# Quarter-array token matmuls for the odd 64 tokens, in a fused attention and MLP-mixer kernel

## The chip, the cores and the metric

The kernel runs on one core of a Trainium2 chip. The metric is the device time of one execution in microseconds, the lower the better.

## The reference

Two stages are computed, for 8 batches of 448 tokens (S) with 12 heads of 64 elements, so 768 features (D). All inputs and the output are float32; the kernel works in float16 with float32 sums.

```python
def _attn_ref(q, k, v):
    S = q.shape[2]
    scale = 1.0 / np.sqrt(q.shape[-1])
    scores = scale * np.matmul(q, k.transpose(0, 1, 3, 2)) - np.log(S)
    attn = 1.0 / (1.0 + np.exp(-scores))
    return np.matmul(attn, v)

def _moe_ref(x, w_tok1, w_tok2, w_ch1, w_ch2):    # x: the heads side by side, 8 x 448 x 768
    xt = x.transpose(0, 2, 1)
    h = np.maximum(xt @ w_tok1, 0.0) @ w_tok2     # 448 -> 256 -> 448 tokens
    u = x + h.transpose(0, 2, 1)
    h2 = np.maximum(u @ w_ch1, 0.0) @ w_ch2       # 768 -> 1536 -> 768 features
    return u + h2
```

## The kernel before

Tokens are loaded so that partition p of 64 holds tokens 7p to 7p+6; a "round" i of attention takes one such j of 7 for two heads. 448 tokens are three and a half tiles of 128: blocks 0 to 2 are full, block 3 has only 64 tokens. In the kernel before, even batches keep that half block in partitions 0 to 63 and odd batches in 64 to 127 (`side`, `ORDER`, `x_block`, `w1_slot`), so that two batches' halves lie in one tile `ut` for the last step.

The work of a batch is:

- attention (`attention`): for each of 3 groups of four heads, 7 rounds S (L587, four matmuls of 64 by 64 array tiles each, into a `wide` PSUM tile), a sigmoid per round on ScalarE (L603), then V (L625, 28 such matmuls into two single banks), and a copy to `xT` on ScalarE (L658). From batch 2 on, q, k and x are transposed by DMAs on SP, after POOL has reordered q and k (L503); in batches 0 and 1 TensorE does it instead (L531 for q and k, L678 for x), and so for x of the last group of batches 2 and 3.
- the first token matmul K1 (`token`, L820): blocks 0 to 3 of x against `w_tok1`, 384 features at a time, followed by a relu on VectorE (L832). Block 3 is a full 128-row matmul although half its rows are blank.
- the second token matmul K2 (L850): for each of 4 blocks and 2 halves of the features two matmuls, then the sum with x on VectorE (L871), a cast on ScalarE (L879) and a DMA transpose into `uT`. Block 3 uses a full tile and only 64 of its output rows.
- the first channel matmul C1 (`channel1`, L927): 12 steps of six matmuls with 448 columns, relu on VectorE (L952) into `h2aT`.
- the second channel matmul C2 (`channel2`): for blocks 0 to 2 12 matmuls per half (L992). For block 3 of two batches together 24 matmuls per half with tiles of 128 by 64 (L1001). Then the sum on VectorE (L1015) and the store.

Batch 0 is different: its token matmuls (K1a L710, KT L744) run piece by piece between its attention groups.

The order of the work is written out by a planner (`Plan.run`, `choose`) when the program is built. Each step has an engine, a planned duration, the steps that it follows and the buffers that it uses. For TensorE the planner picks among the candidates that can start first: an attention visit (two rounds S, at times with a V) when it is due, token steps, then C1, then C2. Each engine then runs its own list in that order. There are four single banks of PSUM (`bank`) for V, K1, K2, C1 and C2, and two double ones (`wide`) for S. A "visit" means a stretch in which the array is in 64 by 64 tiles. `fill` matmuls (L482) keep TensorE going in planned gaps of the first 21 us; the planner has its own model of when loads land (`pipe`).

Of the kernel before, what the change touches and what calls it, by code (L numbers as in the profile page):

```python
# [55 lines left out]
class Plan:  # L56
# [4 lines left out]
    def __init__(self, pools):  # L61
# [4 lines left out]
        self.landed, self.pipe = [0.0] * 8, 0.0  # L66

# [63 lines left out]
    def run(self, choose):  # L131
# [9 lines left out]
        while self.left:  # L141
# [30 lines left out]
            if best is None:  # L172
# [5 lines left out]
                    )[:6000]  # L178
# [4 lines left out]
            if e == "LD":  # L183
                far = self.load_far if self.pipe > 50.0 else 0.4
                free["POOL"] = t + o.n * o.issue
                if self.pipe < 8.6 < free["POOL"] + 1.3 + o.us:
                    self.pipe = 9.6
                self.pipe = max(self.pipe, free["POOL"] + 1.3) + o.us
                o.end = self.pipe + far
# [15 lines left out]
def kernel(  # L205
# [27 lines left out]
    FILL, UP = 21.0, 7  # L233

# [16 lines left out]
    w_tok1 = const("w_tok1", [128, J, TT], FP16)  # L251
    w_tok2_s = const("w_tok2_s", [128, 2, S], FP16)
    w_tok2 = const("w_tok2", [128, 2, 14, P], FP16)
# [5 lines left out]
    ORDER = {0: (0, 4, 1, 5, 2, 6, 3), 1: (3, 4, 0, 5, 1, 6, 2)}  # L259
# [6 lines left out]

    def x_block(side, blk):

        return blk if side == 0 else (blk + 1) % 4

    def mm(n):
        return n / 2400 + 0.003
# [16 lines left out]
    blank = [plan.buf(f"xT{i}", 2, [128, 2, 512], FP16, keep=True) for i in (0, 0, 1, 1)]  # L289

    def zero():
        for i, t in enumerate(blank):
            nc.vector.memset(t[:, :, S:512] if i < 2 else t[:, :, 0 : 512 - S], 0.0)
        for i, t in enumerate(u16_tail):
            nc.vector.memset(t[64:128, :] if i % 2 == 0 else t[0:64, :], 0.0)
# [56 lines left out]
    def load_w_tok1(part):  # L352

        view = moe_w_tok1.rearrange("(p j) t -> p j t", j=J)
        moves = (
            ((0, 0, 0, 4), (64, 0, 4, 3), (64, 3, 3, 1)),
            ((0, 4, 4, 3), (64, 4, 0, 3)),
        )[part]
# [7 lines left out]
        a = op(f"ld_tok1_{part}", "LD", 1.3 if part == 0 else 1.0, emit, uses=[w_tok1])  # L366
# [3 lines left out]
    def load_w_tok2():  # L370
# [8 lines left out]
        for a_, z, j, n in ((0, 6, 0, 3), (1, 6, 4, 3), (6, 8, 3, 1), (8, 14, 4, 3), (9, 14, 0, 3)):  # L379

            def spread(a=a_, z=z, j=j, n=n):
# [6 lines left out]
                op(f"spread{a_}", "DVE", 0.45, spread, [b], [w_tok2_s, w_tok2], rank=-1 if a_ < 7 else 2)  # L388
# [39 lines left out]
    tok1_ld = load_w_tok1(0)  # L428
# [4 lines left out]
    tok1_late = load_w_tok1(1)  # L433
# [55 lines left out]
    def turned(b, m, what, side):  # L489
# [3 lines left out]
        if b >= 2:  # L493
            pm = plan.buf(f"{what}p", 2, [128, J, 2, E], FP16, name=f"{what}p_{b}_{m}")

            def permute():
                src = raw.ap().rearrange("r h j e -> r j h e")
                if side == 0:
                    parts = ((slice(0, 5, 2), slice(0, 3)), (slice(1, 6, 2), slice(4, 7)), (slice(6, 7), slice(3, 4)))
                else:  # L500
                    parts = ((slice(2, 7, 2), slice(0, 3)), (slice(1, 6, 2), slice(4, 7)), (slice(0, 1), slice(3, 4)))
# [675 lines left out]
```

## Time and profile before

| | |
|---|---|
| median of 8 runs | 379.3 us (378.75 to 379.97) |
| profiled execution | 379.58 us |
| its span, first to last instruction | 377.8 us |
| TensorE busy | 369.5 us, 3243 matmuls |
| ScalarE busy | 206.0 us |
| VectorE busy | 164.4 us |
| POOL busy | 116.9 us |
| first channel matmul starts | 38.91 us |
| last matmul ends, last instruction ends | 373.8 us, 377.8 us |
| granted TensorE clock | 0.999 |

A group line of the profile reads: line, engine, operation, output<-input, shape, how many | busy us, mean ns of one | idle time before them and who ended it. [...] the rate is read from start to start in the chain or the timeline. A line of waits reads: who waited, for whom, us in total, how often, the longest.

### The profile page before, as it was taken

To read this page: it belongs to the slowest core of one execution; us is meant where nothing else is said; L and a number is where in the kernel's file an instruction comes from. 1 tells how busy PE (TensorE), PEld (TensorE's weight loads), DVE (VectorE), ACT (ScalarE), POOL (GpSimd) and SP (SyncE) were. 2 spreads that over 40 slices of the span, in tenths; PEclk is the share of its full clock that TensorE was granted. 3 is DMA by queue.
4 is the path that set the end of the run, shared out by engine and by line. 5 is a ranking of instruction groups with operands and counts; after the bars stand their busy time and mean duration, and the time that the engine had idled before them with its cause. 6 is when DMAs were issued, how large, how long until landed. Compare 5 with 4: busy or idle time off the path is not lost.

```text
span 377.8 us, 7941 instructions
## 1 busy us (share of the span) xinstructions
PE 369.5 (98%) x3243; PEld 190.2 (50%) x3243; DVE 164.4 (44%) x308; ACT 206.0 (55%) x251; POOL 116.9 (31%) x263
## 2 busy tenths in 40 slices
PE   8899999999999999999999999999999999999995
PEld 4455454554455554554445555444445565555663
DVE  4485336643353423552342434643432266554221
ACT  5886885476747666776674777954654123000000
POOL 8883226344533325443444433530000000000000
PEclk9999999999999999999999999999999999999999
DMA  7999999999967999999999999993113655200344
GB/s 105 175 167 206 208 208 181 127 222 174 136 107 121 158 183 159 111 148 181 171 134 158 163 185 213 177 147 71 30 16 97 103 113 118 52 2 0 85 100 108
DMA packets 97172, 50.25 MB, mean 133 GB/s; under 512 B 70576, under 2 KB 93616, under 8 KB 97136
## 3 DMA queue, kind: packets, MB, share of 16 engines
q1 hardware_dynamic: 72656, 27.62, 43.1%
q0 software_dynamic: 24240, 21.81, 42.8%
q8 instruction: 25, 0.41, 0.5%
q10 hardware_dynamic: 240, 0.31, 0.2%
q14 instruction: 11, 0.09, 0.1%
HBM read 43.84 MB, written 11.01 MB: 145 GB/s over the span
## 4 chain that ended last, share of the span: by engine, by line
PE 87%; DMA 5%; POOL 4%; ACT 1%; DVE 1%; issue 1%; POOLq 0%; ACTq 0%
PE c L927 27%; PE c L992 25%; PE qk L587 10%; PE xa L625 8%; PE yn L850 5%; PE c L1001 4%; PE k L820 4%; DMA qT<-qp 2%; DMA k<-in_k_dram 2%; DMA uT<-u 1%; POOL k L329 1%; PE k L710 1%; PE xb L678 1%; ACT attn L603 1%; PE tq L531 1%
## 5 line engine op out<-in xcount | busy, mean ns | idle before, releaser
L603 ACT ACTIVATE attn<-qk,att_bias 128x896 f16<-128x896 f32 (+1 forms) x172 | 161.8, 988 | 76.8 <-PE qk L587 76.4
L927 PE MATMUL c<-uT,w_ch 128*128 128x448 f16 x576 | 118.3, 353 | 0.4 <-DMA uT<-u 0.4
L992 PE MATMUL c<-w_ch,h2aT 128*128 128x384 f16 x576 | 98.8, 326 | 0.0
L952 DVE TENSOR_SCALAR h2aT<-c 128x448 f16<-128x448 f32 x96 | 60.0, 625 | 80.7 <-PE c L927 80.5
L927 PEld LDWEIGHTS <-w_ch 128*128 128x128 f16 x576 | 52.9, 98 | 57.5 <-issue 13.5
L992 PEld LDWEIGHTS <-h2aT 128*128 128x128 f16 x576 | 55.2, 98 | 39.9 <-issue 4.5
L1015 DVE TENSOR_TENSOR u<-u,c 128x384 f32<-128x384 f32 x48 | 26.6, 554 | 75.2 <-PE c L992 75.2
L587 PE MATMUL qk<-qT,kT 64*64 64x448 f16 x672 | 52.9, 363 | 1.0 <-DMA qT<-qp 0.3
L625 PE MATMUL xa<-attn,v 64*64 64x448 f16 x672 | 36.7, 350 | 0.0
L784 POOL COPY mark<-attn 1x1 f16<-1x1 f16 x54 | 9.7, 179 | 74.7 <-ACT attn L603 74.7
L587 PEld LDWEIGHTS <-kT 64*64 64x64 f16 x672 | 14.8, 104 | 31.0 <-issue 28.4
L871 DVE TENSOR_TENSOR u<-x,yn 128x384 f32<-128x384 f16 x48 | 24.4, 549 | 9.7 <-PE yn L850 9.5
L879 ACT ACTIVATE u<-u 128x768 f16<-128x768 f32 x21 | 17.8, 846 | 19.9 <-DVE u L871 19.8
L503 POOL COPY qp<-q 128x384 f16<-128x384 f16 (+1 forms) x54 | 21.4, 432 | 22.9 <-DMA q<-in_q_dram 14.6
L850 PE MATMUL yn<-h,w_tok 128*128 128x384 f16 x128 | 26.4, 327 | 0.0
L503 POOL COPY kp<-k 128x384 f16<-128x384 f16 (+1 forms) x54 | 21.3, 431 | 16.2 <-DMA k<-in_k_dram 14.1
L658 ACT ACTIVATE xT<-xa 128x448 f16<-128x448 f32 x43 | 21.1, 547 | 9.4 <-PE xa L625 7.3
L625 PEld LDWEIGHTS <-v 64*64 64x64 f16 x672 | 19.4, 107 | 12.1 <-DMA q<-in_q_dram 0.7
L820 PE MATMUL k<-x,w_tok 128*128 128x384 f16 x112 | 20.2, 327 | 0.2 <-DVE x L696 0.2
L832 DVE TENSOR_SCALAR h<-k 128x384 f16<-128x384 f32 x28 | 15.5, 556 | 9.9 <-PE k L820 8.7
L340 POOL DMA_DIRECT2D q<-in_q_dram x21 | 15.1, 720 | 6.4 <-issue 6.4
L850 PEld LDWEIGHTS <-w_tok 128*128 128x128 f16 x128 | 11.0, 98 | 12.0 <-issue 5.5
(63 smaller groups left out, 187.4 us busy)
## 6 DMA issues: line engine op xcount, KB each, us to landing
out_dram<-u SPq DMA_DIRECT2D x48, 192.0 KB, 3.0
k<-in_k_dram POOLq DMA_DIRECT2D x21, 224.0 KB, 5.2
q<-in_q_dram POOLq DMA_DIRECT2D x21, 224.0 KB, 6.0
v<-in_v_dram POOLq DMA_DIRECT2D x21, 224.0 KB, 5.4
w_ch<-in_moe_w_ch_dram POOLq DMA_DIRECT2D x6, 768.0 KB, 18.7
out_dram<-ut SPq DMA_DIRECT2D x6, 192.0 KB, 5.3
v<-in_v_dram POOLq DMA_DIRECT2D x6, 112.0 KB, 4.9
x<-xT SPq DMA_TRANSPOSE x32, 4.5
```

What stands on the lines that cost most here:

```text
L503: nc.gpsimd.tensor_copy(out=pm[:, to, :, :], in_=src[:, fr, :, :])
L587: nc.tensor.matmul(out=ps[64 * s : 64 * s + 64, h, 0:S], lhsT=kT[64 * h : 64 * h + 64, i, s, :], rhs=qT[64 * h : 64 * h + 64, :, s, :], st ...
L603: nc.scalar.activation(out=at[:, hs, :], in_=ps[:, hs, 0:S], func=SIGMOID, bias=bias_t[:, :], scale=att_scale,)
L625: nc.tensor.matmul(out=ps[s](slice(64 * h, 64 * h + 64)), lhsT=vf[64 * s : 64 * s + 64, h, order[i], :], rhs=attn[i][64 * s : 64 * s + 64, ...
L658: nc.scalar.activation(out=xt[:, s, c0 : c0 + S], in_=ps[s](every), func=COPYF)
L820: nc.tensor.matmul(out=ps[:, :], lhsT=w_tok1[:, w1_slot(side, blk), 128 * t : 128 * t + 128], rhs=X[b][:, x_block(side, blk), c], start=(b ...
L850: nc.tensor.matmul(out=ps[:, :], lhsT=w_tok2[:, t, s0 : s0 + 2, :], rhs=h1[b][:, t, c], start=(t == 0), stop=(t == 1),)
L871: nc.vector.tensor_tensor(out=to, in0=x, in1=y, op=ADD)
L927: nc.tensor.matmul(out=to(), lhsT=w_ch1[cb // 4][:, db, 128 * (cb % 4) : 128 * (cb % 4) + 128], rhs=uT[b][:, db, :], start=(db == 0), stop ...
L952: nc.vector.tensor_scalar(out=h2aT[b][:, cb, :], in0=to(), scalar1=0.0, scalar2=None, op0=MAX)
L992: nc.tensor.matmul(out=ps[:, :], lhsT=h2aT[b][:, cb, 128 * blk : 128 * blk + 128], rhs=w, start=(cb == 0), stop=(cb == NCB - 1),)
L1015: nc.vector.tensor_tensor(out=t, in0=t, in1=ps[:, :], op=ADD)
```

## The change

For batches 2 to 7 (`PACK`) the half block of 64 tokens is stored twice as compactly. ScalarE's copy of the second half of the features writes its last 64 tokens 64 columns further on, so that after the transpose block 3 of `X[b]` holds the first 384 features in partitions 0 to 63 and the other 384 in partitions 64 to 127. With that, block 3 of K1 becomes two steps V1 of four 64 by 64 matmuls each, which open the sums of two banks; K1 then adds three full matmuls to each bank. Block 3 of K2 becomes one step V2 of eight 64 by 64 matmuls; the two halves of the 128 inner rows land in two banks, and VectorE adds both to x, in two additions per half of the features.

V1 and V2 are kept in a list `tails`. The planner appends them to an attention visit when they are ready within 0.05 us of it (and then may take the visit 3 us of work earlier), or issues them alone.

All batches now use the even layout, so the second arrangement of the weights (two DMAs, two copies) goes. C1's relu writes blocks 0 to 2 to `h2aT` and the last 64 tokens to `h2odd`, where those of two batches lie side by side: block 3 of C2 then is 12 full-tile matmuls per half. The planner's model of the loads gets three pauses instead of one. The diff, cut to its core:

```diff
+        self.hitch = [(8.6, 1.1), (15.2, 1.0), (21.9, 0.8)]
...
                 free["POOL"] = t + o.n * o.issue
-                if self.pipe < 8.6 < free["POOL"] + 1.3 + o.us:
-                    self.pipe = 9.6
                 self.pipe = max(self.pipe, free["POOL"] + 1.3) + o.us
+                while self.hitch and self.pipe > self.hitch[0][0]:
+                    self.pipe += self.hitch.pop(0)[1]
                 o.end = self.pipe + far
...
+    PACK = range(2, 8)
+    JOIN, PULL, ALONE = 0.05, 3.0, 3.5
+    PAUSE = 1.0
...
-    w_tok2 = const("w_tok2", [128, 2, 14, P], FP16)
+    w_tok2 = const("w_tok2", [128, 2, 8, P], FP16)
...
-    ORDER = {0: (0, 4, 1, 5, 2, 6, 3), 1: (3, 4, 0, 5, 1, 6, 2)}
+    ORDER = (0, 4, 1, 5, 2, 6, 3)
...
-        moves = (
-            ((0, 0, 0, 4), (64, 0, 4, 3), (64, 3, 3, 1)),
-            ((0, 4, 4, 3), (64, 4, 0, 3)),
-        )[part]
+        moves = ((0, 0, 0, 4), (64, 0, 4, 3), (64, 3, 3, 1))
...
-    tok1_late = load_w_tok1(1)
...
-            xt = plan.buf(f"xT{side}", 2, [128, 2, 512], FP16, name=f"xT_{b}_{m}", keep=True)
+            xt = plan.buf("xT", 4, [128, 2, 512], FP16, name=f"xT_{b}_{m}", keep=True)
...
-                        nc.scalar.activation(out=xt[:, s, c0 : c0 + S], in_=ps[s](every), func=COPYF)
-
-                got.append(op(f"xT_{b}_{m}_{s}", eng, 0.58, take, [vo, zero_op], [ps[s], xt], rank=-3))
+                        nc.vector.tensor_copy(out=xt[:, s, 0:S], in_=ps[s](every))
+                        return
+
+                    packed = b in PACK and s == 1
+                    for to, fr in ((0, 0), (S, S - 64)) if packed else ((0, 0),):
+                        n = S - 64 if fr == 0 and packed else S - fr
+                        nc.scalar.activation(
+                            out=xt[:, s, to : to + n], in_=ps[s](every)[:, fr : fr + n], func=COPYF
+                        )
+
+                got.append(op(f"xT_{b}_{m}_{s}", eng, 0.75 if b in PACK and s else 0.58, take, [vo, zero_op], [ps[s], xt], rank=-3))
             cols = head_cols(b, m)
...
+            need = [x for m in range(NQ) for x in x_ops[(b, m)]]
+            for n, c in enumerate(cuts) if b not in PACK else ():
...
+            for t in range(2) if b in PACK else ():
+                pair = [bank(f"k1_{b}_{n}_{t}", [128, DH]) for n in range(2)]
+
+                def odd1(pair=pair, t=t):
+                    for n, c in enumerate(cuts):
+                        for g in range(2):
+                            z = slice(128 * t + 64 * g, 128 * t + 64 * g + 64)
+                            nc.tensor.matmul(
+                                out=pair[n][64 * g : 64 * g + 64, :],
+                                lhsT=w_tok1[64 * n : 64 * n + 64, 3, z],
+                                rhs=X[b][64 * n : 64 * n + 64, 3, c],
+                                start=True,
+                                stop=False,
+                                skip_group_check=True,
+                            )
+
+                odd = op(f"V1_{b}_{t}", "PE", mm(DH), odd1, [*need, tok1_ld], [*pair, X[b], w_tok1, h1[b]])
+                odd.kind = "64"
+                tails.append(odd)
+                for n, c in enumerate(cuts):
+
+                    def tok1(ps=pair[n], c=c, t=t):
+                        for blk in range(3):
+                            nc.tensor.matmul(
+                                out=ps[:, :],
+                                lhsT=w_tok1[:, blk, 128 * t : 128 * t + 128],
+                                rhs=X[b][:, blk, c],
+                                start=False,
+                                stop=(blk == 2),
+                                skip_group_check=True,
+                            )
+
+                    o = op(f"K1_{b}_{n}_{t}", "PE", 3 * mm(DH), tok1, [odd], [pair[n], X[b], w_tok1, h1[b]])
+                    first.append(o)
...
+            if b in PACK and blk == 3:
+                pair = [bank(f"yt_{b}_{n}", [128, DH]) for n in range(2)]
+
+                def odd2(pair=pair):
+                    for t in range(2):
+                        for n in range(2):
+                            for g, c in enumerate(cuts):
+                                z = slice(64 * n, 64 * n + 64)
+                                nc.tensor.matmul(
+                                    out=pair[n][64 * g : 64 * g + 64, :],
+                                    lhsT=w_tok2[z, t, 6, :],
+                                    rhs=h1[b][z, t, c],
+                                    start=(t == 0),
+                                    stop=(t == 1),
+                                )
+
+                o = op(f"V2_{b}", "PE", 2 * mm(DH), odd2, [*relus, *tok2_ld], [*pair, h1[b], w_tok2, utile, u16])
+                o.kind = "64"
+                tails.append(o)
+
+                sums = o
             for half, c in enumerate(cuts):
+                if sums:
+
+                    def add(half=half, c=c, pair=pair):
+                        z = slice(64 * half, 64 * half + 64)
+                        to = utile[r, :].rearrange("t (g s e) -> t s g e", s=2, e=E)[:, half]
+                        x = X[b][z, 3, c].rearrange("t (g e) -> t g e", e=E)
+                        for y in pair:
+                            y = y[z, :].rearrange("t (g e) -> t g e", e=E)
+                            nc.vector.tensor_tensor(out=to, in0=x, in1=y, op=ADD)
+                            x = to
+
+                    adds.append(op(f"u_{b}_3_{half}", "DVE", 0.96, add, [sums], [*pair, utile, X[b]], rank=-2))
+                    continue
...
-        h2aT[b] = plan.buf("h2aT", 2, [128, NCB, S], FP16, name=f"h2aT_{b}")
+        h2aT[b] = plan.buf("h2aT", 2, [128, NCB, S - 64], FP16, name=f"h2aT_{b}")
+        if b % 2 == 0:
+            h2odd[b // 2] = plan.buf("h2odd", 2, [128, NCB, 2, 64], FP16, name=f"h2odd_{b // 2}")
+        odd = h2odd[b // 2]
...
+            def relu(cb=cb, ps=ps):
+                for to, fr in ((h2aT[b][:, cb, :], slice(0, S - 64)), (odd[:, cb, b % 2, :], slice(S - 64, S))):
+                    nc.vector.tensor_scalar(
...
+            ch1_ops[b].append(op(f"h2_{b}_{cb}", "DVE", 0.74, relu, [o], [ps, h2aT[b], odd], rank=-2))
...
                         if blk < 3:
-                            nc.tensor.matmul(
-                                out=ps[:, :],
-                                lhsT=h2aT[b][:, cb, 128 * blk : 128 * blk + 128],
-                                rhs=w,
-                                start=(cb == 0),
-                                stop=(cb == NCB - 1),
-                            )
+                            h = h2aT[b][:, cb, 128 * blk : 128 * blk + 128]
                         else:
-                            for s in range(2):
-                                nc.tensor.matmul(
-                                    out=ps[64 * s : 64 * s + 64, :],
-                                    lhsT=h2aT[b - 1 + s][:, cb, 384:448],
-                                    rhs=w,
-                                    start=(cb == 0),
-                                    stop=(cb == NCB - 1),
-                                )
+                            h = h2odd[b // 2][:, cb, :, :]
+                        nc.tensor.matmul(
+                            out=ps[:, :], lhsT=h, rhs=w, start=(cb == 0), stop=(cb == NCB - 1)
+                        )
...
+        if any(o.name[:3] == "V2_" for o in c[2]):
+            state["rest"] = -PAUSE
...
+                more = []
+                for o in tails[:3]:
+                    r2 = plan.ready(*g[2], *more, o) if g[0] else None
+                    if r2 is not None and r2 <= max(t, r) + JOIN:
+                        more.append(o)
+                        r = max(r, r2)
+                p = -1 if g[0] == 0 else 1 if state["done"] >= due(g) - (PULL if more else 0) else 5
+                cands.append((max(t, r), p, g[2] + more, "64", groups, g))
+        if tails and (ALONE or not groups):
+            alone = []
+            for o in tails[:3]:
+                r = plan.ready(*alone, o)
+                if r is not None and r <= t + 0.3:
+                    alone.append(o)
+            if alone:
+                cands.append((max(t, plan.ready(*alone)), ALONE or 1.5, alone, "64", [0], 0))
```

## The prediction

> **What bounds the kernel now.** I read the page's busy shares first, then the chain that ended last, then the waits of TensorE, then the groups by form, then the timeline of the start.
>
> ```profile
> PE 369.5 (98%) x3243; PEld 190.2 (50%) x3243; DVE 164.4 (44%) x308; ACT 206.0 (55%) x251; POOL 116.9 (31%) x263
> ...
> PE 87%; DMA 5%; POOL 4%; ACT 1%; DVE 1%; issue 1%; POOLq 0%; ACTq 0%
> ```
>
> TensorE (PE) is busy 98% of the span and is 87% of the chain; the other engines are near half. A busy PE could still be one that waits inside, so the waits come next.
>
> ```profile
> PE idle L467 <- DVE att_bias L276: 1.2, 1, 1.2
> PE tk L531 <- DMA k<-in_k_dram: 0.9, 1, 0.9
> PE c L927 <- DMA uT<-u: 0.4, 1, 0.4
> ```
>
> These are the three largest waits of PE in the whole run; two lie in the first 18 us. After that PE runs its program back to back, so what counts is the length of that program: streaming time plus the cost of changing the shape of the array. The chain in time order gives both (start, duration, what).
>
> ```profile
> 97.43 2.38 PE c L927 x12
> 99.81 0.50 PE qk L587 x8
> 100.31 1.24 PE c L927 x6
> ...
> 277.89 1.32 PE xa L625 x28
> ...
> 320.26 26.10 PE c L927 x138
> 346.36 23.40 PE c L992 x144
> 369.76 4.04 PE c L1001 x48
> ```
>
> Rates without a change of shape: 26.10/138 = 0.189 us for a full-tile matmul of 448 columns, 23.40/144 = 0.1625 us for 384 columns. The attention values (xa, 64 by 64 tiles, four at a time) take 1.32/28 = 0.047 us each, a quarter of 0.189: quarter tiles overlap fully, so one of 384 columns should take 0.1625/4 = 0.041 us. L1001, two 128 by 64 tiles at a time, takes 4.04/48 = 0.084 us each, so two of them (0.168) cost slightly more than one full tile. A change of shape: six c matmuls between two visits take 1.24 against 6 x 0.189 = 1.135, and a visit of eight qk takes 0.50 against 8 x 0.047 = 0.38; together 0.23 us for entering and leaving a visit, 0.115 us a change.
>
> [...] 0.115 us a change, while xa directly behind qk shows none (1.32). [...] The trace has 0.625 us for 448 and 0.556 us for 384 columns; that slope gives 0.21 us, which I use.
>
> **The change, part by part.** The durations that I use besides those above:
>
> ```profile
> L952 DVE TENSOR_SCALAR h2aT<-c 128x448 f16<-128x448 f32 x96 | 60.0, 625 | 80.7 <-PE c L927 80.5
> L832 DVE TENSOR_SCALAR h<-k 128x384 f16<-128x384 f32 x28 | 15.5, 556 | 9.9 <-PE k L820 8.7
> L871 DVE TENSOR_TENSOR ut<-x,yn 64x384 f32<-64x384 f16 x16 | 8.2, 548 | 1.8 <-PE yn L850 1.6
> ```
>
> *Token matmuls of batches 2 to 7.* First: 16 full matmuls of 384 columns become 12 and 8 quarters. Second: the four of block 3 become 8 quarters. Per batch 8 x 0.1625 = 1.30 leave and 16 x 0.041 = 0.65 come: 0.65 saved, six batches 3.9 us. This is on the path, since PE is.
>
> *Last channel matmul.* 192 half-width ones at 0.084 (16.2) become 96 full ones at 0.1625 (15.6): 0.5 us saved.
>
> *Changes of shape.* I counted them in both built programs' order of PE instructions, from the first channel matmul on: 159 before, 164 after. Of the 18 new quarter steps 12 ride in a visit, at no change; 6 stand alone (the second half of batches 2, 3, 4, all three of batch 7), 12 changes. Gone are those around the 128 by 64 tiles. Net +5 x 0.115 = +0.6 us. One pair of second token matmuls of batch 0 also moves from the start into this stretch: +0.3.
>
> Sum after the start: -3.9 - 0.5 + 0.6 + 0.3 = -3.5 us.
>
> *VectorE.* Each of 96 channel relus becomes 0.556 + 0.21 = 0.77 us (+0.14); two sums a batch become four (+2 x 0.55). That is +14 and +6.6 us on 164 busy. I cost it at nothing: a channel step gives VectorE at least 6 x 0.189 = 1.13 us per relu. Without that cover, it would be 0.14 us for each of 96.
>
> *ScalarE.* 18 copies of 448 columns (0.547) are split in 384 and 64 columns; by the slope to the 846 ns copy of 768 columns, 0.49 + 0.19, so +0.13 each, 2.4 us on 206. Behind them are queued sigmoids (1.0 us) and, on SP, the transposes of x; ScalarE idles 76 us for qk, which hides it.
>
> *New waits.* A first token step now needs all of a batch's x, not its half; in batches 4 to 7 the order puts 7 us or more of PE work between the last xa and it, against a 4.5 us transpose and up to 2 us of ScalarE (2 and 3 turn their last group on PE). The second quarter step keeps two of the four single banks until four sums are done: 4 x 0.55 + 0.2 = 2.4 us. In the new order PE comes back to one of those banks only after 2.8 us or more in batches 2, 3, 4, 6 and 7. In batch 5 the step follows xa in the same visit, so all four banks are taken. The next c waits for ScalarE to finish two sigmoids and one xa copy, about 2.4 + 0.55 us after the visit began, where PE gets there at 2.5: 0.5 us. The same step's path to batch 5's first c (sums 2.4, cast up to 2, transpose 5.0) is about as long as the 8.0 us of PE work before it plus that 0.5 us; the uT wait above (0.4) is of this kind. I book +0.5 us for all, between -0.4 (only that wait goes) and +3.
>
> *The start.* Two weight DMAs for the odd order and two copies go; the scheduler's model of load landings changes, so the order changes.
>
> ```profile
> 15.91 0.38 PE L587 MATMUL qk<-qT,kT 64*64 64x448 f16 x4
> 17.24 0.58 PE L531 MATMUL tk<-ident,k 128*64 128x128 f16 x14 [0.95 <-DMA k<-in_k_dram]
> ...
> 18.41 1.01 ACT L603 ACTIVATE attn<-qk,att_bias 128x896 f16<-128x896 f32 x1 [1.05 <-PE qk L587]
> ```
>
> Batch 0 runs at ScalarE's pace of one sigmoid a microsecond, and here it lost 1.05 us: PE stood at tk for a load, with the next qk queued behind it. In the new order that qk and the xb transposes go first. The price: the k and q transposes of batch 1's second group (28, about 1.0 us) now stand behind the last xa of batch 0, where PE is closer to the path; they partly fill its waits there. Followed step by step with the durations of before, the first c (38.9 us before) starts about 1 us earlier. I take -1.0, between -2.0 and +0.3. The removed DMAs took about 1.1 us of landing time (the last load before them lands at 20.4 us, the second of them at 21.5), so the loads behind come earlier too and the next stage is not starved. The end (4 us from the last matmul) is unchanged.
>
> **Sum.** -3.5 + 0.5 - 1.0 = -4.0 us. The profiled execution took 379.6 us (span 377.8 and 1.8 around it), so 375.6; it lies 0.3 above the median of the runs, 379.3. I predict 375.4 us.
>
> **The rivals.**
> *The start gives nothing* (or the waits eat as much): the transposes moved behind xa cost what the gap gave. 375.4 + 1.0 = 376.4. For it: that stretch of PE is nearly full. Chance 0.22.
> *A late uT:* batch 5's last transpose comes 2 to 3 us late, or the bank waits repeat at other places; the matmul saving stays. About 378. For it: the uT wait already there; against: those 8.5 us of cover. Chance 0.15.
> *Slower, by the banks:* every second quarter step stalls PE because two of four banks are gone for 2.4 us while sums and relus queue on VectorE. A stall of 0.9 us at each of six, and 0.2 at each of 12 first ones, is 7.8 us: 375.4 - 0.5 + 7.8 = 382.7. It decides from a mean of about 0.8 us per second step, that is, where PE's cover is under 1.6 us; the order has that in one batch of six. Chance 0.08.
> *The change doesn't do what it says:* quarters do not overlap, 96 x 0.12 us more, 387. Against: xa at 47 ns. Chance 0.02.
> *Better:* the start gains 2 us and no wait is added, 373.9. Chance 0.05.
> The forecast itself has 0.48, with its own range 374.3 to 376.2.
>
> **How the numbers follow.** Below 374.2 lie about 0.06 (the better case), above 378.4 about 0.14 (the two slower rivals and the worst of the late uT); that is the range. A measurement of this kernel tells about 0.2% (0.8 us) from no change. Faster: all of the forecast, the start's rival and the better case, and 0.10 of the late uT: 0.85. Within 0.2%: its other 0.05. Slower: 0.10, the two slower rivals.
>
> **What would show it.** First token matmuls x72 and quarters x48 and x48 at about 41 ns start to start; channel matmuls all 0.1625; the first c near 37.9 us; PE's waits near 1 us after the start; VectorE near 185 us busy. Wrong would be: c or xa waiting on VectorE sums (banks), c waiting on uT over 1 us, or a first c later than 38.9 us.

## The result, and the profile after

The changed kernel takes 375.63 us (median of 11 runs, 374.92 to 376.99) against 379.19 us for the kernel before in the same session: a ratio of 0.9904, 95% interval 0.9886 to 0.9922. Two more executions on record, 377.16 and 379.99 us, are not in that median; with them it is 375.82. The change takes 3.6 us off, where 4.0 were forecast, and the time lies 0.2 us from the predicted one. The profiled execution took 375.96 us with a span of 374.2 (before: 379.58 and 377.8).

The page of the changed kernel, its busy times and its chain by engine:

```profile
PE 367.2 (98%) x3199; PEld 187.4 (50%) x3199; DVE 176.3 (47%) x414; ACT 207.4 (55%) x269; POOL 116.1 (31%) x261
...
PE 92%; DMA 3%; POOL 2%; DVE 1%; issue 1%; ACT 0%; POOLq 0%
```

TensorE still bounds the kernel, and more so: it is 92% of the chain, from 87%. VectorE rose by 12 us, not by the 21 that the prediction summed, ScalarE by 1.4 in place of 2.4; both are still near half.

The waits of TensorE (for whom, us in total, how often, the longest):

```profile
PE idle L463 <- DVE att_bias L276: 1.2, 1, 1.2
PE c L997 <- DMA uT<-u: 0.4, 1, 0.4
PE qk L578 <- ACT qT L547: 0.3, 1, 0.3
PE qk L578 <- ACT uT L761: 0.3, 1, 0.3
```

The 0.9 us of tk (the transposes of k on TensorE) for a load, the second largest wait of before, is gone. The uT wait is as large as it was, but it is another batch's (batch 3 at 180 us; before it was at 255 us).

The groups by form, with those that the change made or altered:

```profile
L1011 DVE TENSOR_SCALAR h2aT<-c 128x384 f16<-128x384 f32 x96 | 53.5, 557 | 81.2 <-PE c L997 81.1
L1011 DVE TENSOR_SCALAR h2odd<-c 128x64 f16<-128x64 f32 x96 | 20.5, 214 | 0.0
L1054 PE MATMUL c<-w_ch,h2odd 128*128 128x384 f16 x96 | 16.6, 326 | 0.0
L857 PE MATMUL k<-x,w_tok 128*128 128x384 f16 x72 | 13.8, 328 | 0.0
L841 PE MATMUL k<-x,w_tok 64*64 64x384 f16 x48 | 4.1, 333 | 0.0
L891 PE MATMUL yt<-h,w_tok 64*64 64x384 f16 x48 | 3.0, 324 | 0.0
```

The counts are the forecast ones: 72 full first token matmuls, 48 and 48 quarters. A mean of 324 to 333 ns says nothing of a matmul's rate: the records overlap, since full tiles of 384 columns with 326 ns each start 162 to 163 ns apart. The rate comes from start to start. Four quarters start 3 to 4 ns apart, and the next four of the same step follow 152 to 153 ns after the fourth (177 once, behind a change of shape). So four V1 take 0.1625 us, and a change of shape when a full tile follows (0.265), eight V2 0.325 and the change (0.428). That is 41 ns each.

For all kernels below I split the profiled execution at two points: the start of the first channel matmul (first c), and the start of the last matmul. Between them lies the stretch; "rates" is the sum of the rates of all its matmuls and 0.115 us for each change of shape; "rest" is the stretch less that sum, so waits and the error of the rates. Half-width tiles are counted at 0.1625 us a pair here (see the half-width experiment). Ratios are to the kernel before, from the timed runs. The kernels e1 to e12 ran after the changed kernel, each beside the kernel before again (medians 379.0 to 379.4 us); with the intervals of both ratios, the distance of each from the changed kernel is known to about 1 us.

| kernel | median us | ratio, 95% interval | first c | changes of shape | stretch | rates | rest |
|---|---|---|---|---|---|---|---|
| before | 379.19 | 1 | 38.91 | 159 | 334.55 | 333.0 | 1.5 |
| after | 375.63 | 0.9904, 0.9886 to 0.9922 | 38.30 | 164 | 331.56 | 330.0 | 1.6 |
| e1_nopack | 377.44 | 0.9953, 0.9936 to 0.9970 | 37.58 | 154 | 333.50 | 332.8 | 0.7 |
| e2_alone | 378.65 | 0.9984, 0.9969 to 0.9999 | 37.65 | 176 | 334.23 | 331.4 | 2.8 |
| e3_before_newload | 378.11 | 0.9969, 0.9958 to 0.9979 | 37.92 | 160 | 334.14 | 333.4 | 0.7 |
| e4_after_oldload | 380.69 | 1.0048, 1.0016 to 1.0080 | 41.30 | 164 | 336.45 | 329.7 | 6.8 |
| e5_c2half | 375.92 | 0.9911, 0.9892 to 0.9930 | 37.81 | 169 | 331.71 | 330.6 | 1.1 |
| e6_hold | 378.90 | 0.9987, 0.9967 to 1.0008 | 37.91 | 164 | 340.69 | 330.0 | 10.7 |
| e7_v2apart | 378.46 | 0.9990, 0.9966 to 1.0014 | 37.84 | 168 | 333.80 | 330.5 | 3.3 |
| e8_pack1 | 380.88 | 1.0043, 1.0028 to 1.0057 | 37.99 | 168 | 337.96 | 329.8 | 8.2 |
| e9_relu3 | 376.10 | 0.9927, 0.9907 to 0.9946 | 38.80 | 164 | 333.18 | 330.0 | 3.2 |
| e10_v2apart_due | 377.05 | 0.9954, 0.9934 to 0.9974 | 38.23 | 168 | 332.81 | 330.5 | 2.4 |
| e11_pause0 | 376.45 | 0.9935, 0.9911 to 0.9959 | 37.72 | 162 | 333.39 | 329.8 | 3.6 |
| e12_holdlate | 378.78 | 0.9989, 0.9967 to 1.0011 | 37.79 | 164 | 334.56 | 330.0 | 4.6 |

Medians and ratios leave out the few runs on record as slow (381.87 us beside a median of 376.45 in e11_pause0, for one), and the profiled executions of e4_after_oldload (383.9 us), e6_hold (384.7), e8_pack1 (382.1) and e9_relu3 (378.1) lie 3, 6, 1 and 2 us above these medians, so their stretches say where waits are, not how long a median run is.

### The profile page after: what moved, and what is told of

Read it like the earlier page. It is cut to its first block, busy times and chain, and to the rows that moved or that the text cites. A ratio compares the mean times of both kernels' runs of the same rounds, so it can differ in the third digit from the quotient of the medians.

```text
span 374.2 us, 7987 instructions
## 1 busy us (share of the span) xinstructions
PE 367.2 (98%) x3199; PEld 187.4 (50%) x3199; DVE 176.3 (47%) x414; ACT 207.4 (55%) x269; POOL 116.1 (31%) x261
## 4 chain that ended last, share of the span: by engine, by line
PE 92%; DMA 3%; POOL 2%; DVE 1%; issue 1%; ACT 0%; POOLq 0%
PE c L997 30%; PE c L1054 29%; PE qk L578 10%; PE xa L616 8%; PE yn L923 5%; PE k L857 3%; DMA w_tok_s<-in_moe_w_tok_dram 2%; DMA uT<-u 1%; PE xb L675 1%; POOL k L329 1%; PE k L707 1%; PE k L817 1%; PE k L841 1%; PE tk L524 1%; POOL q L329 1%; PE yt L891 1%
## 5 line engine op out<-in xcount | busy, mean ns | idle before, releaser
L1011 DVE TENSOR_SCALAR h2aT<-c 128x384 f16<-128x384 f32 x96 | 53.5, 557 | 81.2 <-PE c L997 81.1
L1064 DVE TENSOR_TENSOR u<-u,c 128x384 f32<-128x384 f32 x48 | 26.6, 554 | 64.6 <-PE c L1054 64.5
L653 ACT ACTIVATE xT<-xa 128x448 f16<-128x448 f32 (+2 forms) x61 | 22.2, 440 | 9.7 <-PE xa L616 8.4
L496 POOL COPY qp<-q 128x384 f16<-128x384 f16 (+1 forms) x54 | 21.4, 433 | 11.9 <-DMA q<-in_q_dram 10.4
L923 PE MATMUL yn<-h,w_tok 128*128 128x384 f16 x104 | 22.0, 327 | 0.1
L1011 DVE TENSOR_SCALAR h2odd<-c 128x64 f16<-128x64 f32 x96 | 20.5, 214 | 0.0
L340 POOL DMA_DIRECT2D v<-in_v_dram x21 | 15.2, 722 | 5.9 <-issue 2.2
L1054 PE MATMUL c<-w_ch,h2odd 128*128 128x384 f16 x96 | 16.6, 326 | 0.0
```

The source lines that it names most:

```text
L340: nc.gpsimd.dma_start(out=t.ap().rearrange("r h j e -> r h (j e)"), in_=heads.rearrange("(h s) (p j) e -> (s p) h (j e)", s=2, j=J),)
L496: nc.gpsimd.tensor_copy(out=pm[:, to, :, :], in_=src[:, fr, :, :])
L653: nc.scalar.activation(out=xt[:, s, to : to + n], in_=ps[s](every)[:, fr : fr + n], func=COPYF)
L923: nc.tensor.matmul(out=ps[:, :], lhsT=w_tok2[:, t, s0 : s0 + 2, :], rhs=h1[b][:, t, c], start=(t == 0), stop=(t == 1),)
L1011: nc.vector.tensor_scalar(out=to, in0=ps[:, fr], scalar1=0.0, scalar2=None, op0=MAX)
L1054: nc.tensor.matmul(out=ps[:, :], lhsT=h, rhs=w, start=(cb == 0), stop=(cb == NCB - 1))
```

## The experiments

**Which part gives what.** Three kernels, each with one part of the change in another state. First, no quarter steps; the even layout, the full-tile last step and the new load model stay:

```diff
-    PACK = range(2, 8)
+    PACK = range(0)
```

> The changed kernel with no batch packed: block 3 of both token matmuls is done with full tiles again in all batches; the even layout, the shared tile in the last channel matmul and the new load model stay. From the first channel matmul on, the order of instructions has 24 more full token matmuls each side (+7.8 us), no quarters (-3.9), 10 changes of shape fewer (-1.15), 0.6 us fewer or more for one moved pair and for waits. Theory (the quarter tiles give most of the gain): about +2.3 us on the changed kernel, 377.9. Rival (the channel tile and the start give most of it): within 0.8 us of the changed kernel, under 376.5.

Measured: 377.44, 1.8 us more than the changed kernel. Its stretch is 1.9 us longer. So the quarters give 1.9 net: their matmuls save 3.9, the ten changes of shape that they bring (154 to 164) take 1.15 back, and the rest grows by 0.8 (0.7 to 1.6).

Second, the kernel before with the planner's new model of the loads and nothing else:

```diff
+        self.hitch = [(8.6, 1.1), (15.2, 1.0), (21.9, 0.8)]
...
-                if self.pipe < 8.6 < free["POOL"] + 1.3 + o.us:
-                    self.pipe = 9.6
                 self.pipe = max(self.pipe, free["POOL"] + 1.3) + o.us
+                while self.hitch and self.pipe > self.hitch[0][0]:
+                    self.pipe += self.hitch.pop(0)[1]
```

> The kernel before with only the planner's new model of load landings (three pauses in place of one); all weights in both layouts are still loaded. Theory (the start gains by the order, since qk no longer stands behind a wait for a load): the wait of 0.9 us at tk goes and the first channel matmul starts near 38.3 us in place of 38.9; one pair of token matmuls moves behind it (+0.3): the time is 0.3 to 0.6 us below the kernel before. Rival (the removed weight loads gave the start): first channel matmul at 38.9, time unchanged.

Measured: 378.11, 1.2 us less than before (interval 0.8 to 1.6), twice the upper end of what I expected. The timeline of TensorE has its first channel matmul here, 0.99 us earlier than before:

```profile
37.92 1.31 PE L928 MATMUL c<-uT,w_ch 128*128 128x448 f16 x6
```

The wait of tk for a load is not in its list any more. So the start's gain is a matter of the order alone; the two weight DMAs and copies that the change takes away are still there. In the profiled executions another 0.4 us comes from the stretch: this order has no wait for uT, and its rest is 0.7 us in place of 1.5.

Third, the changed kernel with the old model of the loads, that is, those lines reversed:

> The changed kernel with the planner's old model of load landings. Theory (order): the first channel matmul starts at 38.9 again, the stretch behind is 0.3 us shorter (one pair of token matmuls moves back): +0.3 us on the changed kernel, 375.9. Rival (removed loads): the start stays at 38.3 and the time is 0.3 us below the changed kernel.

Measured: 380.69, 5 us more than the changed kernel where I expected almost nothing. The waits of TensorE:

```profile
PE c L997 <- issue: 2.1, 1, 2.1
PE tk L524 <- DMA k<-in_k_dram: 2.0, 1, 2.0
```

The second is the start's wait again, doubled, and behind it the granted clock of TensorE was at half from 19.7 to 23.1 us (first c at 41.30). The first is at 344.59 us, far from anything that a load touches: a change in the first 20 us of the plan gave another order for the whole run. In this order only 4.1 us of TensorE work lie between batch 7's last K2 and its first channel matmul, 10.4 us in the changed kernel; the transpose into uT isn't there by then: it was issued at 343.72 and took 3.2 us to land, to 346.9, and the matmul starts at 347.02. "issue" in such a line names no releaser; the landing does. The expectation missed that a planner's variants differ in places which the edit doesn't touch.

**The half-width tiles.** The changed kernel, with the last channel step of block 3 in tiles of 128 by 64 again:

```diff
-                            h = h2odd[b // 2][:, cb, :, :]
+                            for s in range(2):
+                                nc.tensor.matmul(
+                                    out=ps[64 * s : 64 * s + 64, :],
+                                    lhsT=h2odd[b // 2][:, cb, s, :],
+                                    rhs=w,
+                                    start=(cb == 0),
+                                    stop=(cb == NCB - 1),
+                                )
+                            continue
```

> The changed kernel, but block 3 of the last channel matmul again in 128 by 64 tiles, two at a time, reading the same shared buffer. 192 matmuls at 0.084 us in place of 96 at 0.1625 (+0.57) and 5 more changes of shape (+0.58). Theory: +1.15 us, 376.8. Rival (half tiles cost nothing beside full ones): within 0.3 us of the changed kernel.

Measured: 375.92, 0.3 more, with intervals that overlap; the rival was right. Start to start the two matmuls of a pair stand 3 to 4 ns apart and the next pair follows 0.1625 us after the first, to the nanosecond what a full tile takes; only the first pair behind a change of shape takes 24 ns more. The prediction's 0.084 us came from a row of the chain that runs to the end of its last matmul, 0.3 us behind that one's start. So the 96 full tiles save nothing against 96 pairs. What is left are five more changes of shape, 0.6 us by the price above. Against them, the profiled execution of the changed kernel has one wait for uT (0.47 us, at 180 us) which that of this one doesn't have. 0.6 - 0.5 is 0.1; the stretch grew by 0.15.

**Riding in a visit.** Quarter steps are never appended to a visit:

```diff
-                    if r2 is not None and r2 <= max(t, r) + JOIN:
+                    if r2 is not None and r2 <= max(t, r) - 1000.0:
```

> The changed kernel, but the planner may never append a quarter step to a visit; each is issued alone. The order has the same matmuls and 176 changes of shape in place of 164. Theory (0.115 us a change, nothing else): +1.4 us, 377.0. Rival (riding in a visit is what makes the banks short, so apart is as good): 375.6 or less.

Measured: 378.65, 3.0 more than the changed kernel, twice what 12 more changes of shape (1.4 us) account for. The waits of TensorE show the other half:

```profile
PE qk L578 <- ACT attn L594: 1.5, 2, 1.0
...
PE c L997 <- DMA uT<-u: 0.2, 1, 0.2
```

Visits now stand too close behind each other at 267 to 271 us, and the next qk waits for a sigmoid. Not every step is alone, either: six of the 18 still fall directly behind a visit, which is why there are only 12 more changes. Joining is worth 1.4 us by that count; the rest belongs to the order that resulted.

**One more batch.** Quarter steps in batch 1 too:

```diff
-    PACK = range(2, 8)
+    PACK = range(1, 8)
```

> The changed kernel with batch 1 packed as well. Full matmuls of one batch leave, quarters come (-0.65), four more changes of shape (+0.46). Theory: -0.2 us and whatever the new waits take, so within 0.4 us of the changed kernel; batch 1's first step now waits for all of its x and stands alone, so a wait there of 0.3 us is likely. Rival (each packed batch gives a net 0.6 us as the six others): 375.0.

Measured: 380.88, 5.3 more. The rates sum is 0.2 lower, as it should be, and the rest is 8.2:

```profile
PE qk L578 <- ACT attn L594: 1.4, 3, 0.5
PE c L997 <- DVE u L1064: 1.2, 1, 1.2
PE ut L966 <- ACT u L953: 1.2, 1, 1.2
...
PE xa L616 <- DVE ut L913: 0.6, 1, 0.6
```

Here is a wait of the kind that the slower rival was about, xa for the four sums (ut L913), once. But more comes from two other places. Around 88 us, in a stage where TensorE still transposes for itself, it waits for a cast (1.2) and for sigmoids (0.4 and 0.5), and then its granted clock (PEclk) is at half for 3.4 us:

```profile
core 0: us, PE busy (x) PEld busy (x) DVE busy (x) ACT busy (x) POOL busy (x), PEclk, DMA share, GB/s
90.72:94.13 3.41, 3.03 (x32) 1.56 (x31) 0.00 (x0) 2.12 (x3) 2.52 (x6) 0.50 1.10 217
```

By an estimate from those 3.41 us at half, that is up to 1.7 us more, which no list of waits shows. The other place is batch 7's first channel matmul. Its wait of 1.2 is put down to a sum (DVE u L1064), but that sum had ended 0.6 us before:

```profile
345.73 0.55 DVE L1064 TENSOR_TENSOR u<-u,c 128x384 f32<-128x384 f32 x1 [1.32 <-PE c L1054]
346.90 1.29 PE L997 MATMUL c<-uT,w_ch 128*128 128x448 f16 x6 [1.20 <-DVE u L1064]
```

The transpose into uT, issued at 343.66, took 3.1 us to land, to 346.8. So it is the late uT again, with the same short cover of 4.1 us as in the kernel with the old load model.

**The banks.** Two kernels hold the pair of banks of each second quarter step longer. The first has a copy on VectorE after each half's sums:

```diff
                             nc.vector.tensor_tensor(out=to, in0=x, in1=y, op=ADD)
                             x = to
+                        nc.vector.tensor_copy(out=spare[z, :], in_=pair[1][z, :])
```

> The changed kernel with one more VectorE copy of 64 by 384 out of the second bank after each pair of sums of block 3, into a buffer that nothing reads: the two banks are held 1.1 us longer in each of six batches (3.5 us in place of 2.4), the order of TensorE's work is the same. Theory (PE comes back to those banks after 2.8 us or more in five of six): 0.6 us in batch 2, 0.7 in batch 6, 0.3 in batch 7, up to 1 for the later uT of batch 5: +1.5 to +2.5, about 377.6. Rival (the banks bind at every second step): +1.1 in each of six, +6.6, 382.

Measured: 378.90, 3.3 more than the changed kernel. Its profile shows two things. TensorE waited for the copies (0.7, 0.6 and 0.2 us), and 4.5 us for batch 3's uT; the copies also stood ahead of the sums of the second half, so cast and transpose were later. On SP that transpose came behind others in one queue (start, duration, what):

```profile
169.27 3.30 SPq L1040 DMA_DIRECT2D out_dram<-u  x2
172.66 2.42 SPq L502 DMA_TRANSPOSE qT<-qp  x1
175.17 2.54 SPq L665 DMA_TRANSPOSE x<-xT  x2
177.81 1.26 SPq L983 DMA_TRANSPOSE uT<-u  x1
```

In the changed kernel the last of these starts at 174.97. I took the late uT for the main cause, and the next kernel tests that: both copies stand after all four sums, so that the banks are held as long but the cast isn't delayed.

```diff
                             nc.vector.tensor_tensor(out=to, in0=x, in1=y, op=ADD)
                             x = to
+                        for y in pair * half:
+                            nc.vector.tensor_copy(out=spare[:, :], in_=y[:, :])
```

> The changed kernel with two copies of a whole bank (0.55 us each) on VectorE after the last of the four sums of every second quarter step: both of its banks are held 1.1 us longer, as in the kernel with a copy after each half, but the cast and the transpose into uT no longer stand behind a copy. Theory (what made that kernel 3.3 us slower was the late uT of one batch, and the bank pair itself has 1 us of slack in most batches): within 1.2 us of the changed kernel, 376 to 376.8. Rival (the banks are what hurts): 378 or more, with TensorE waiting for the copies at every second quarter step.

Measured: 378.78, again 3.2 more. The theory fell. Its waits:

```profile
PE xa L617 <- DVE spare L917: 0.9, 1, 0.9
PE c L1057 <- DVE spare L917: 0.9, 1, 0.9
...
PE c L1000 <- DMA uT<-u: 0.4, 1, 0.4
```

The order of all 3199 matmuls is that of the changed kernel, so the two can be laid over each other start by start. The stretch is 3.0 us longer: 1.02 at the second quarter step of batch 2, 1.01 at batch 6's, 0.75 in three pieces at batch 7's; the uT waits add 0.2. At batches 3, 4 and 5 the longer hold costs nothing. The rival was wrong in "every", right in size.

So where was the slack in the changed kernel? TensorE around batch 6's step:

```profile
286.06 0.49 PE L891 MATMUL yt<-h,w_tok 64*64 64x384 f16 x8
286.49 1.31 PE L997 MATMUL c<-uT,w_ch 128*128 128x448 f16 x6
287.73 0.38 PE L578 MATMUL qk<-qT,kT 64*64 64x448 f16 x4
288.04 1.31 PE L997 MATMUL c<-uT,w_ch 128*128 128x448 f16 x6
289.19 1.14 PE L1054 MATMUL c<-w_ch,h2aT 128*128 128x384 f16 x6
```

And VectorE in the same stretch:

```profile
286.59 0.55 DVE L913 TENSOR_TENSOR ut<-x,yt 64x384 f32<-64x384 f16 x1
287.24 0.55 DVE L913 TENSOR_TENSOR ut<-ut,yt 64x384 f32<-64x384 f32 x1
287.82 0.56 DVE L913 TENSOR_TENSOR ut<-x,yt 64x384 f32<-64x384 f16 x1
288.41 0.56 DVE L913 TENSOR_TENSOR ut<-ut,yt 64x384 f32<-64x384 f32 x1
```

The pair is taken at 286.06 and the last sum ends at 288.97: 2.9 us. TensorE writes to one of its banks at 289.19. At batch 2 the same two times are 119.52 and 119.82, at batch 7 314.27 and 314.67. That is 0.2 to 0.4 us of slack, at three of the six, less the hand-over itself: in the kernel with the two copies TensorE started 0.05 and 0.15 us after the last copy had ended.

**VectorE's load alone.** The 64-column part of every channel relu is written twice; nothing else changes in the order:

```diff
-                for to, fr in ((h2aT[b][:, cb, :], slice(0, S - 64)), (odd[:, cb, b % 2, :], slice(S - 64, S))):
+                for to, fr in ((h2aT[b][:, cb, :], slice(0, S - 64)), (odd[:, cb, b % 2, :], slice(S - 64, S)), (odd[:, cb, b % 2, :], slice(S - 64, S))):
```

> The changed kernel with the 64-column part of every channel relu written twice: 96 more VectorE operations of 0.214 us (the mean of the same operation in the changed kernel), 20.5 us in all, in the same order on every engine. Theory (a channel step gives VectorE 1.13 us for a relu of 0.77, so its extra work is covered): within 0.4 us of the changed kernel, about 375.8, and first relu-bound waits of TensorE stay absent, although a relu is now 0.99 us. Rival (VectorE already hands on late what the transposes into uT wait for, so that each added 0.2 us in its queue shows): 377 or more, with TensorE waiting for uT in the trace.

Measured: 376.10; the ratio's interval overlaps that of the changed kernel (0.9907 to 0.9946 against 0.9886 to 0.9922), the fastest run is at 375.22. VectorE is busy for 197.8 us in place of 176.3, and that cost 0.5 us by the medians, 0.9 by the ratios: not clearly more than nothing. The profiled execution at 378.07 us has one large wait, for batch 4's uT:

```profile
227.62 0.57 PE L578 MATMUL qk<-qT,kT 64*64 64x448 f16 x8
229.92 1.29 PE L997 MATMUL c<-uT,w_ch 128*128 128x448 f16 x6 [1.72 <-DMA uT<-u]
```

SP's queue in this kernel:

```profile
220.79 1.90 SPq L981 DMA_TRANSPOSE uT<-u  x1
222.78 3.81 SPq L664 DMA_TRANSPOSE x<-xT  x2
```

And in the changed kernel:

```profile
220.44 1.42 SPq L981 DMA_TRANSPOSE uT<-u  x1
221.95 2.73 SPq L664 DMA_TRANSPOSE x<-xT  x2
```

It was issued 0.35 us later and landed after 9.0 us in place of 6.0. Here VectorE is not what came late; the transposes themselves took longer.

**The step that holds all four banks.** In batch 5 the second quarter step follows xa in one visit. This kernel keeps such steps apart:

```diff
+        state["hadv"] = row is groups and any(o.name[:2] == "V_" for o in c[2])
...
+                    if o.name[:2] == "V2" and (state.get("hadv") or any(x.name[:2] == "V_" for x in g[2])):
+                        continue
...
+                if o.name[:2] == "V2" and state.get("hadv"):
+                    continue
```

> The changed kernel, but a second quarter step is not taken in or right behind a visit with attention values, so the four single banks are never all taken by the two. In batch 5 it rides two rounds later; four more changes of shape (+0.5). Theory (the 0.5 us that PE lost behind that visit is the banks): that wait goes, the total stays within 0.3 us of the changed kernel. Rival (the wait is the sigmoid's hold of the wide bank alone): the wait stays, +0.5 us.

Measured: 378.46, 2.8 more. The wait at batch 5 is gone, and another is there. (In the changed kernel it is 0.3 us rather than 0.5, and both explanations have a share: 0.15 us by a qk that starts at 259.36, where the second sigmoid ends at 259.31, and 0.13 by a c at 259.79, where the first xa copy ends at 259.74.)

```profile
336.73 4.06 PE L1054 MATMUL c<-w_ch,h2aT 128*128 128x384 f16 x24
342.58 5.65 PE L997 MATMUL c<-uT,w_ch 128*128 128x448 f16 x29 [1.79 <-issue]
```

That is batch 7's first channel matmul once more, with a cover of 4.1 us; its transpose was issued at 339.31 and landed 3.2 us later, at 342.5. To see if this short cover is the cause, the next kernel adds to this one an earlier due time for batch 7's attention, which puts the cover back to 10.4 us at the same 168 changes of shape:

```diff
-        return -1.0 if b < 2 else base[b - 1] - LEAD + i * SPAN * mix[b - 1]
+        return -1.0 if b < 2 else base[b - 1] - LEAD - 3 * (b == 7) + i * SPAN * mix[b - 1]
```

> As the kernel with the second quarter step kept out of visits that hold a V (378.5 us), but the attention of batch 7 is due 3 us of work earlier. Its order of TensorE's instructions has the same 168 changes of shape; between batch 7's last K2 and its first channel matmul lie 10.4 us of TensorE work in place of 4.1. Theory (those 378.5 came from that short cover, 2.1 us of waiting for uT, not from keeping the step apart): about 376.3, with no wait over 1 us for uT after 330 us. Rival (keeping the step apart costs by itself): 378 or more still.

Measured: 377.05, between the two expectations: 1.4 of the 2.8 us came back. Its waits:

```profile
PE c L997 <- DMA uT<-u: 0.8, 1, 0.8
...
PE yn L923 <- DVE u L1064: 0.4, 1, 0.4
```

The wait at the end is gone, as the theory said; the two that are left are at 227 us (batch 4's uT) and 300 us (a bank). So the cover is the cause of that one wait. A separate step isn't better by itself: it costs four changes (0.46) and takes away 0.3 us of waiting.

**A shorter order.** Another setting of one of the planner's constants gives two changes of shape fewer and keeps 8 us of TensorE work or more in front of the first channel matmul of batches 3 to 7:

```diff
-    PAUSE = 1.0
+    PAUSE = 0.0
```

> The changed kernel with the planner's constant PAUSE at 0 in place of 1: two changes of shape fewer (162), and TensorE work of 8 us or more ahead of the first channel matmul of batches 3 to 7. Theory (the sum of matmul rates and changes of shape sets the time where that cover is long): 0.2 to 0.3 us below the changed kernel, 375.3. Rival (another order brings other waits): 376 or more.

Measured: 376.45, 0.8 more than the changed kernel by the medians, 1.2 by the ratios. The intervals overlap, so a loss isn't clear, but no gain is there. In the profiled execution a cover of 9.6 and 11.1 us of TensorE work did not suffice for batches 3 and 4, so the theory's "long" was too short:

```profile
PE c L997 <- issue: 1.2, 1, 1.2
...
PE c L997 <- DMA uT<-u: 0.8, 1, 0.8
```

These are at 227 us (batch 4, whose transpose took 7.6 us to land, to 228.8, where the matmul starts at 228.9) and 176 us (batch 3). For batch 4 the order isn't all of it: the changed kernel has the same cover there, about 11 us, and no wait, because its transpose was issued 0.8 us earlier and landed after 6.0 us; with the relu written twice, in the same order, it landed after 9.0. No version that I ran beats the changed kernel.

## Why the prediction was right, step by step

- *Token matmuls, -3.9.* Right: counts and the 41 ns are as forecast. The quarters of one group start 3 to 4 ns apart, and 41 ns is the mean of four. The kernel without quarters shows what is left of the term after its ten changes of shape and the waits of the new order, 1.9 us.
- *Last channel matmul, -0.5.* This term was mis-sized: a pair of half-width tiles takes the 0.1625 us of a full one, so it is 0. The 0.084 us were misread from a row that includes the end of its last matmul. The full tiles pay by the changes of shape that they save, which the next term has.
- *Changes of shape, +0.6, and the moved K2 pair, +0.3.* The counts (159 and 164) are those of the runs. With them the sum of the rates falls by 3.0 us, not 3.5.
- *New waits, +0.5.* The rest stayed as it was, 1.5 and 1.6 us. The place was right: batch 5's step with xa costs time at 259 us, though 0.3 us and not 0.5, and 0.3 came at 121 us (yn). But others went: 0.35 of a qk at 70 us, and 0.57 for uT at 255, for which 0.47 came at 180, at batch 3 and not at batch 5, where the prediction had looked. The net is about +0.1. The stretch is 3.0 us shorter, as -3.5 + 0.5 had it, but by luck: two errors of 0.4 to 0.5 cancelled.
- *The banks' cover.* The step behind "only after 2.8 us or more" against a hold of 2.4 us was too comfortable: the hold is 2.9 us or more, because the first sum starts 0.5 us or more after the step does, and TensorE returns after 3.1 to 3.6 us. It held by 0.2 to 0.4 us at three places. That a quarter step needs a pair of banks was the author's premise, and no run has one with a single bank; the kernels that hold the pair 1.1 us longer show what it costs when the cover is used up, 3 us. The slower rival's mechanism was real, with a price of 0.75 to 1 us at three steps for 1.1 us of lateness; the forecast escaped it by a narrow margin.
- *VectorE and ScalarE at nothing.* Right within what the runs can tell. VectorE's sum was too high: the small relu of 64 columns takes the 0.21 us of the prediction's slope (0.214 measured; 0.625 for 448 columns and 0.556 for 384 gave it), but it starts 0.08 us before the recorded end of the large one (283.97 against 283.49 + 0.56), so the two take 0.69 us together and not 0.77. 96 x (0.69 - 0.625) and 6.6 for the sums are 12.8, near the 11.9 of the page.
- *The start, -1.0.* Right for its reason: the new model of the loads alone, put on the kernel before, moves the first c by -0.99 us. In the profiled execution of the changed kernel the gain is 0.6: a weight load landed late there, VectorE's copy of it began at 16.13 us (15.13 in the kernel with half-width tiles, whose start is the same), the casts of xT queue behind that copy, and a qk began 0.5 us later. The other kernels with the new model have their first c at 37.6 to 38.2, but for the one with the relu written twice, which shows the same wait for xT (0.8 us).
- *The end, unchanged.* 4.3 us from the last matmul's start to the end in both.

0.6 and 3.0 make the 3.6 us between the two profiled executions. (The prediction's own sum gives 375.3 us, 0.1 below the 375.4 that it states.) By the ratios of the experiments the 3.6 us fall apart in another way: the planner's load model alone gives 1.2, the even layout with the full tiles of the last step some 0.6, and the quarter tiles 1.9, each uncertain by 0.4 to 0.9 us. So the quarters, which the change is named after, are about half of the gain.

The chance of 0.15 for a late uT was not too high: each of the six variants of the changed kernel whose order of the quarter steps or of the start differs (e2, e4, e7, e8, e10, e11) has at least one wait of 0.8 us or more, and in five of them the longest in the stretch is for uT, at batch 4 or 7.

## What to carry to other kernels

Quarter tiles pay what their count says (here 41 ns each for 384 columns), less the changes of shape (0.115 us each), and both can be read off the order of instructions before any run; what cannot be read off is the waits of the order, which here left a rest of 0.7 to 10.7 us. So judge an order by its covers: for each hand-over (matmul, sum, cast, queue, transpose) the work that its consumer's engine has meanwhile, and for each buffer how long it is held from the first write to the last read, with the reader's queue counted in. A cover with only 0.2 us to spare is invisible in a profile, because nothing waits; holding the buffer 1 us longer, as a test, makes it visible. Where a wait is put down to an instruction that had ended well before, or to none ("issue"), look at what landed just before the wait's end: here that was a transpose into uT in four kernels.

## What the runs showed of the hardware

The same transpose into uT (batch 4's last), issued at nearly the same time (220.44 and 220.79 us) beside the same two others, landed after 6.0 us in one execution and 9.0 in another. Batch 7's last one, where attention's transposes are done, landed after 3.1 to 3.2 us in the three kernels that waited for it. With batch 4's 3 us later, in the kernel with the relu written twice, TensorE waited 1.72 us for it; whether such landings are most of the spread between runs, no run shows.

Some waits of TensorE were followed by slower matmuls. In the kernel with the copies after each half, TensorE stood for 4.45 us, and the matmuls of 448 columns behind that took 373 ns from start to start in place of 189:

```profile
185.06 4.62 PE L999 MATMUL c<-uT,w_ch 128*128 128x448 f16 x12 [4.45 <-DMA uT<-u]
```

With the old load model, nine such slow matmuls (1.7 us more) came behind a wait of 2.10 us, 2.43 us from start to start; behind one of 1.79 us, 2.12 us from start to start, in the kernel with the step kept apart there were none. The granted clock goes with them: between 8 us and the last matmul the traces show it at half in four stretches, of 3.41 us or of twice that: two with the old load model (19.71 to 23.12 and 347.39 to 350.80 us), one with batch 1 packed (90.72 to 94.13) and one with the copies after each half (182.72 to 189.54). In the 3.41 us ahead of each, TensorE was busy for 1.3 to 1.7 us. With batch 1 packed no single wait there was longer than 1.2 us (columns as in the line of that kernel above):

```profile
87.31:90.72 3.41, 1.72 (x20) 0.80 (x19) 1.62 (x4) 2.70 (x4) 2.03 (x5) 1.00 1.26 226
```

So the clock was at half behind a stretch with no wait above 1.2 us, and not behind a wait of 1.79 us: the length of one wait doesn't decide it, and what does, these runs don't show.
